# A cached attention decode step with a small MLP: the order of the three weight loads and of the products on them, and the place of TensorE's wait at the end of its group loop

## The chip, the cores and the metric

The kernel runs on one core of a Trainium2 chip. The metric is the device time of one execution in microseconds (us). TensorE (PE in the profile, with its sequencer PEq and its weight loads PEld) does the matrix products, VectorE (DVE) transposes, reductions and elementwise work, ScalarE (ACT) the exponentials and other functions, GpSimd (POOL) small set-up and copies, and SyncE (SP) issues nearly all DMAs, in order, on one queue.

## The reference, cut to what matters

```python
xn = _layernorm(x)                               # x: 2 x 1 x 512
q = (xn @ wq)                                    # 32 heads of 128
scores = einsum("bhqd,bhkd->bhqk", q, k) * (Dh ** -0.5)   # caches: 2 x 8 heads x 32768 x 128, bf16
p = _softmax(scores)
o = einsum("bhqk,bhkd->bhqd", p, v)
s = o.reshape(B, Sq, Hq * Dh) @ wo
# the MLP on xn; with one token the first two products meet only shifted-in zeros,
# so x1 = xn and w1, w2 are not needed
h2 = _gelu(_layernorm(x1) @ w3) @ w4             # w3: 512 x 1792, w4: 1792 x 512
out = x + s * _silu(x1 + h2)
```

The K and V caches are 128 MB each (16 pairs of batch and KV head, 8 MB each for K and V), and every byte is read once.

## The kernel before

**Groups.** A group is one pair of batch and KV head; there are NG = 16. For each group 8 MB of K and 8 MB of V are loaded. K lies in kbuf, which has three slots of 4 MB: even groups use slots 0 and 1, odd ones 1 and 2, so that a new K can start when the first half of the group before is done. V lies in vbuf, one buffer of 8 MB.

**One group.** VectorE transposes K in 16 pieces (L621) into four buffers T and gives one credit on the semaphore `t_vt` for each. TensorE takes two credits at a time (L728, the helper `take` of L404: wait until the semaphore has n, then subtract n), and multiplies each piece with the group's q columns (`z`, L733), in an inner loop of two halves (L725). Then come the head of the group before (`head_xp`, L700), the row maxima of VectorE (`peak`, L600) and their exchange (L743), the exponentials of ScalarE (L523), their transposes on VectorE (L640), the products with V (L755), the sums (L762), ScalarE's copy of the result to `ob` (L528), and four products that turn it (`head_oT`, L694). `fill` (L707) is an idle product whose result nobody reads. The normalising of a group (`head_on`, L575 to L584, ending with the tile `on`) is done by VectorE within the next group, or, after the last group, at once.

**The loop on TensorE.** The body `pe_groups` (L723 to L768) ends with the products of `head_oT` and a compare-and-branch (L768) with a prefetch hint placed at the body's start (L724). The first thing behind the branch is the inner loop's set-up and the take of two credits on `t_vt`. After the last group TensorE falls through to `pe_output` (L771): it waits for VectorE's `oX_sp` and the last copies of `oX`, does the product `wide` (L773), one fill, takes one credit that VectorE gives with `on` (L586), does `head_xp` and then the products with `wo` (L793, L801), which arrive in six parts.

**What orders the DMAs.** SyncE issues in program order: w3 (L325), wq (L326), w4 (L327), the first K (L328), two small pieces of x (L345), the first V (L482, once `e_h2`, the last product on w4, is done, since w3 and w4 lie in vbuf), four small copies of g (L491), then in turn K of the next group (L500, when TensorE has begun the last piece of the first half, which also says that slot's transposes are done) and V of the next group (L482, when TensorE is done with V of the group before, as ScalarE tells at L527). K and V of the last group are split into halves (L505, L486), and the parts of wo follow (L513, L515). The first K-group that overwrites wq's slot also waits for `e_q`.

**The prologue.** After two layernorms (VectorE, with ScalarE's square roots) four small transposes (L409) give `xT`. Then, in this order on TensorE: 16 products on w3 (the gate, L418), q's 32 products on wq in a loop of eight (L439), 14 products on w4 (L468, L462, L470), and one product that spreads q (L471). On VectorE: the transpose of the gate's products (L422) and the gelu's steps up to `h_bf` (L430, with ScalarE's tanh at L428), q's 16 transposes (L450), `q_sb` (L453), the copy `qr` (L474), from which GpSimd makes `z`, and then the silu `g` (L476, L478) and four memsets (L492 to L495), after which the groups begin.

Of the kernel before, what the change touches and what calls it, by code (L numbers as in the profile page):

```python
# [10 lines left out]
ACT = mybir.ActivationFunctionType  # L11
ALU = mybir.AluOpType
# [10 lines left out]
GELU_C = 0.7978845608028654  # L23
# [108 lines left out]
def kernel(  # L132
# [28 lines left out]
    NB = Dh // 64  # L161
# [5 lines left out]
    NQ = 4  # L167
# [46 lines left out]
    sel = sb("sel", [128, 4, 32], BF16)  # L214
# [107 lines left out]
    with tc.tile_critical(sync_engine=mybir.EngineType.Pool, no_gpsimd_drain=True):  # L322
        nc.scalar.wait_ge(t_shift, n_out).then_inc(t_shift, -n_out)

        sp.op(lambda e: e.dma_start(out=vbuf[:, 0:W4O], in_=B_w3.rearrange("(p k) f -> p (k f)", k=DK)), inc=(d_w3, 16))  # L325
        sp.op(lambda e: e.dma_start(out=kbuf_wq[:, 0:DK * HD], in_=A_wq.rearrange("(p k) f -> p (k f)", k=DK)), inc=(d_wq, 16))  # L326
# [77 lines left out]
        def take(eng, s, n=1):  # L404
            eng.wait_ge(s, n).then_inc(s, -n)  # L405

        treg = qrb[:, :].bitcast(BF16)
        for k in range(DK):
# [2 lines left out]
        e_xT = ve.op(lambda v: v.tensor_copy(  # L411
            out=xT[:, :, :].rearrange("p (s k) b -> p s k b", s=2),
            in_=treg[:, 0:64 * DK].rearrange("p (k s c) -> p s k c", k=DK, s=2)[:, :, :, 0:B]), e)
        FQ = Fdim // NQ
        for k in range(DK):
            for n in range(NQ):
                last = k == DK - 1 and n == NQ - 1
                e = pe.op(lambda t, k=k, n=n: t.matmul(  # L418
                    pro[32 * n:32 * n + B, 0:FQ], lhsT=xT[:, DK + k, :],
                    rhs=w3v[:, k, n * FQ:(n + 1) * FQ].rearrange("p (y f) -> p f y", y=32),  # L420
                    start=(k == 0), stop=(k == DK - 1), tile_position=(0, 32 * n)), e_xT, (d_w3, 16), e_pro0, inc=last)
        e = ve.op(lambda v: v.transpose(out=h4[:, :], in_=pro[:, 0:FQ]), e)  # L422
        e_hf = ve.op(lambda v: v.tensor_copy(
            out=hf[:, :].rearrange("p (f b) -> p f b", b=B), in_=h4[:, :].rearrange("p (f c) -> p f c", c=32)[:, :, 0:B]), e)
        e = ve.op(lambda v: v.tensor_mul(out=x2[:, :], in0=hf[:, :], in1=hf[:, :]), e_hf)
        e = ve.op(lambda v: v.tensor_scalar(out=x2[:, :], in0=x2[:, :], scalar1=0.044715, scalar2=1.0, op0=ALU.mult, op1=ALU.add), e)
        e = ve.op(lambda v: v.tensor_mul(out=inner[:, :], in0=hf[:, :], in1=x2[:, :]), e)
        e = ac.op(lambda v: v.activation(out=th[:, :], in_=inner[:, :], func=ACT.Tanh, scale=GELU_C), e)  # L428
        e = ve.op(lambda v: v.tensor_scalar(out=th[:, :], in0=th[:, :], scalar1=0.5, scalar2=0.5, op0=ALU.mult, op1=ALU.add), e)
        e_hb = ve.op(lambda v: v.tensor_mul(out=h_bf[:, :], in0=hf[:, :], in1=th[:, :]), e)  # L430
        HC = 512 // Dh
        NC = Hq // HC
        QP2 = 2 * HC
# [12 lines left out]
        for c in range(NC // 2):  # L446
# [7 lines left out]
            out=q_sb[:, :, :, :].rearrange("p n e (b h) -> p (n e) b h", b=B),  # L454
            in0=qT[:, :].rearrange("p (h c) -> p c h", c=32)[:, 0:B, :].unsqueeze(1).broadcast_to([128, 2 * NB, B, Hq]),
            in1=cls[:, :, :].rearrange("p n e -> p (n e)").unsqueeze(2).unsqueeze(3).broadcast_to([128, 2 * NB, B, Hq])), e)
        h2 = pro
        W4N = 2

        def w4_part(t, j):  # L460
# [7 lines left out]
        pe.op(lambda t: t.matmul(h2[0:B, :], lhsT=h_bf[:, 0:B], rhs=w4v[:, 0, :], start=True, stop=False), e_hb, (d_w4, 16), inc=False)  # L468
        pe.loop(nc, (FK - 2) // W4N, w4_part)
        e_h2 = pe.op(lambda t: t.matmul(h2[0:B, :], lhsT=h_bf[:, (FK - 1) * B:FK * B], rhs=w4v[:, FK - 1, :], start=False, stop=True))  # L470
        e = pe.op(lambda t: t.matmul(  # L471
            qrb[:, 0:NB * 2 * B * Hq], lhsT=sel[:, :, :].rearrange("p j w -> p (j w)"),
            rhs=q_sb[:, :, :, :].rearrange("p n e c -> p (n e c)"), start=True, stop=True), e_q, e_sel)
        e_qr = ve.op(lambda v: v.tensor_copy(  # L474
            out=qr[:, :, :, :, :].rearrange("p n e b h -> p (n e b h)"), in_=qrb[:, 0:NB * 2 * B * Hq]), e)
# [98 lines left out]
        def head_on(c, par=0, behind=None):  # L574
            nc.vector.tensor_reduce(  # L575
                out=den[:, :], in_=S[:, 0:NPART * rep].rearrange("p (i h) -> p h i", h=rep),
                axis=AX.X, op=ALU.add).wait_op(*sum_of(par), "sem-ge").then_inc(*c.inc(t_d))
            nc.vector.reciprocal(out=rec[:, :], in_=den[:, :]).wait_op(*c.at(t_d), "sem-ge").then_inc(*c.inc(t_d))
            nc.vector.tensor_mul(
                out=recm[:, :, :], in0=rec[:, :].unsqueeze(1).broadcast_to([128, NQ, rep]),  # L580
                in1=sel_h[:, :].unsqueeze(2).broadcast_to([128, NQ, rep])).wait_op(*c.at(t_d), "sem-ge").then_inc(*c.inc(t_d))
            e = c.at(t_d)
            nc.vector.wait_ge(*out_of(par))
            ins = nc.vector.tensor_mul(  # L584
                out=on[:, :, :], in0=oT[:, :].unsqueeze(1).broadcast_to([128, NQ, rep]), in1=recm[:, :, :]).wait_op(*e, "sem-ge")
            ins.then_inc(t_vt if behind else t_on, 1)  # L586
            if behind:
                behind()

# [101 lines left out]
        def head_oT():  # L691
            take(nc.tensor, t_ob)
            for t in range(VT):
                ins = nc.tensor.matmul(  # L694
                    oT[:, :], lhsT=ob[:, t * Dh:(t + 1) * Dh], rhs=sel_o[:, t, :],
                    start=(t == 0), stop=(t == VT - 1))
# [26 lines left out]
        with nc.body("pe_groups", valid_engines=[PE]):  # L723
# [44 lines left out]
            nc.tensor.br_lt(turn, NG, on_true="pe_groups", on_false="pe_output").branch_hint(hint_p)  # L768


        with nc.body("pe_output", valid_engines=[PE]):  # L771
            pe.wait(e_sp, e_oX[NG - 2])
            pe.op(lambda t: t.matmul(  # L773
                wide, lhsT=sel_w[:, :, :].rearrange("p j w -> p (j w)"), rhs=oX_sp[:, :, :, :, :].rearrange("p k b j r -> p (k b j r)"),
                start=True, stop=True))
            fill(1)
            take(nc.tensor, t_vt)
            head_xp()
            for i, (a, c, r0, r1) in enumerate(wo_parts):
                if i == 5:  # L780
                    for n in range(NQ):
# [61 lines left out]
```

## Time and profile before

| what | value |
|---|---|
| median of 3 runs | 657.43 us (655.94, 657.43, 1017.87) |
| the profiled execution, its own time | 658.3 us |
| its span, first to last instruction | 656.5 us |
| mean granted TensorE clock | 0.876 |
| TensorE products, busy | 433.2 us (66%) |
| VectorE, busy | 387.6 us (59%) |
| ScalarE, busy | 39.7 us (6%) |
| DMA packets of SyncE's queue | 280.50 MB, 98.8% of 16 engines' span |

The profiled execution took 658.3 us, 1.8 us more than its span, and lies 0.9 us above the median of the runs. The third run of the row, 1017.87 us, left no profile. A timeline row in the fences below gives the start in us, the duration in us, the engine, the line of the kernel, the operation with its tiles, and in brackets how long the engine had been idle and what ended that. PEq, SPq and ACTq are the sequencers of those engines. A row "DMA to landing" gives the time from an issue's start to the arrival of the last byte.

### The profile page before, as it was taken

How to read it: one execution, taken by the hardware profiler on the slowest of the kernel's cores; microseconds unless marked ns; L12 is line 12 of the kernel's file. 1: busy time of each engine (PE TensorE's matmuls, PEld its weight loads, DVE VectorE, ACT ScalarE, POOL GpSimd, SP SyncE). 2: the span in 40 equal slices, each digit the busy share in tenths (PEclk: the TensorE clock that was granted, in tenths of full speed). 3: DMA queues.
4: the chain of work that ended last, by engine and by line, in shares of the span. 5: the costliest groups of instructions: out<-in, count | busy, mean ns of one | idle time of the engine just before them, and what ended most of it. 6: DMA issues, size and time to landing. Idle time of an engine off the chain costs nothing. (4 is left out here: it accounts for less than half of the span.)

```text
span 656.5 us, 6538 instructions
## 1 busy us (share of the span) xinstructions
PE 433.2 (66%) x2443; PEld 161.9 (25%) x2443; DVE 387.6 (59%) x554; ACT 39.7 (6%) x90; POOL 10.3 (2%) x44
## 2 busy tenths in 40 slices
PE   2737587575858756585775658677574866757975
PEld 0212222222322212232222223222222322222322
DVE  5568293763829367381945739185572918548861
ACT  1010101000010100001010000100000010000100
POOL 1000000000000000000000000000000000000000
PEclk9869889697988969799796988979698996969998
DMA  8999999999999999999999999999999999999995
GB/s 361 437 447 447 435 427 415 447 447 435 423 419 447 447 435 415 427 447 447 435 415 427 447 443 439 415 427 447 439 443 411 431 447 435 447 407 429 431 426 236
DMA packets 6245, 280.52 MB, mean 427 GB/s; under 512 B 730, under 2 KB 868, under 8 KB 1380
## 3 DMA queue, kind: packets, MB, share of 16 engines
q1 hardware_dynamic: 6232, 280.50, 98.8%
q8 instruction: 1, 0.02, 0.0%
q10 hardware_dynamic: 12, 0.00, 0.0%
HBM read 280.50 MB, written 0.00 MB: 427 GB/s over the span
## 5 line engine op out<-in xcount | busy, mean ns | idle before, releaser
L621 DVE STREAM_TRANSPOSE T<-kbuf 128x1024 int32<-128x1024 int32 x256 | 296.5, 1214 | 169.7 <-DMA kbuf<-in_A_k_cache_dram 159.5
L733 PE MATMUL banks<-T,z 128*128 128x512 bf16 x1024 | 276.7, 424 | 163.2 <-PEq L405 161.1
L733 PEld LDWEIGHTS banks<-T,z 128*128 128x128 bf16 x1024 | 99.6, 104 | 333.5 <-issue 245.8
L755 PE MATMUL banks<-vbuf,pt 128*16 128x512 bf16 x1024 | 70.4, 379 | 17.7 <-PEq L405 17.7
L523 ACT ACTIVATE ep<-banks,shift 128x512 bf16<-128x512 f32 x32 | 21.7, 682 | 494.6 <-ACTq L405 494.6
L755 PEld LDWEIGHTS banks<-vbuf,pt 128*16 128x16 bf16 x1024 | 27.3, 88 | 64.9 <-issue 42.7
L600 DVE TENSOR_REDUCE mx<-banks 128x1 f32<-128x512 f32 x32 | 21.5, 672 | 34.4 <-PE xp L700 34.4
L707 PE MATMUL pro<-ob,comb 128*2 128x512 f32 x66 | 33.7, 592 | 0.0
L640 DVE STREAM_TRANSPOSE pt<-ep 128x512 bf16<-128x512 bf16 x32 | 22.7, 708 | 15.0 <-ACT ep L523 15.0
L743 PE MATMUL banks<-mxr,same_h 128*128 128x448 f32 x32 | 15.8, 577 | 18.3 <-PEq L405 18.3
L694 PEld LDWEIGHTS oT<-sel_o,ob 128*128 128x128 f32 x128 | 15.5, 191 | 11.1 <-issue 11.1
L694 PE MATMUL oT<-sel_o,ob 128*128 128x4 f32 x128 | 16.4, 252 | 0.0
L762 PE MATMUL banks<-sm,ones_f 128*128 128x448 f32 x32 | 16.3, 593 | 0.0
L528 ACT COPY ob<-banks 128x512 f32<-128x512 f32 x16 | 9.4, 585 | 78.6 <-ACTq L405 78.6
L439 PE MATMUL banks<-kbuf,xT 128*2 x32 | 9.4, 440 | 4.7 <-PEq L405 3.3
L632 DVE TENSOR_REDUCE shift<-banks 128x1 f32<-128x64 f32 x16 | 3.6, 225 | 14.3 <-PE banks L743 14.3
L545 POOL COPY oX<-oXs 128x4 bf16 (+1 forms) x16 | 3.0, 186 | 552.2 <-POOLq L405 552.2
L450 DVE STREAM_TRANSPOSE T<-banks 32x256 f32<-32x256 f32 x16 | 7.0, 440 | 6.7 <-PE banks L439 6.3
L743 PEld LDWEIGHTS banks<-mxr,same_h 128*128 128x128 f32 x32 | 4.8, 188 | 22.6 <-issue 22.6
L604 DVE TENSOR_SCALAR mxr<-row_of,mx 128x32 f32<-128x32 f32 x32 | 7.7, 242 | 1.1
L707 PEld LDWEIGHTS pro<-ob,comb 128*2 128x2 f32 x66 | 4.2, 84 | 14.0 <-issue 10.4
L409 PE MATMUL qrb<-ident,xs_bf 34*128 34x34 bf16 x4 | 0.3, 198 | 9.9 <-DVE xs_bf L369 9.9
(102 smaller groups left out, 87.4 us busy)
## 6 DMA issues: line engine op xcount, KB each, us to landing
kbuf<-in_A_k_cache_dram SPq DMA_DIRECT2D x2, 4096.0 KB, 22.3
vbuf<-in_A_v_cache_dram SPq DMA_DIRECT2D x2, 4096.0 KB, 21.7
kbuf<-in_A_wq_dram SPq DMA_DIRECT2D x1, 4096.0 KB, 16.7
vbuf<-in_B_w_dram SPq DMA_DIRECT2D x2, 1792.0 KB, 14.0
kbuf<-in_A_wo_dram SPq DMA_DIRECT2D x1, 2048.0 KB, 30.7
kbuf<-in_A_wo_dram SPq DMA_DIRECT2D x3, 512.0 KB, 31.8
kbuf<-in_A_wo_dram SPq DMA_DIRECT2D x1, 384.0 KB
kbuf<-in_A_k_cache_dram SPq DMA_DIRECT2D x15, 27.0
```

The costliest lines, as they stand in the source:

```text
L439: ins = t.matmul(out_c, lhsT=xT[:, k, :], rhs=wq3[:, k, bass.ds(c * 512, 512)], start=(k == 0), stop=(k == DK - 1))
L523: nc.scalar.activation(out=ep[i][:, :], in_=sc[i][:, :], func=ACT.Exp, scale=inv_sqrt_dh, bias=shift[:, :], accum_out=rs[:, i:i + 1]).then ...
L528: nc.scalar.copy(out=ob[:, :], in_=o[:, :]).then_inc(t_ob, 1)
L600: ins = nc.vector.tensor_reduce(out=mx[:, i:i + 1], in_=sc[i][:, :], axis=AX.X, op=ALU.max)
L621: ins = nc.vector.transpose(out=Ts[n % T_BUFS][:, :].rearrange("p (b t k) -> p t b k", b=NB, t=RT), in_=kt[:, r * W:(r + 1) * W].rearrange ...
L640: ins = nc.vector.transpose(out=pt[h][:, :, :].rearrange("p r (t h) -> p t r h", h=rep), in_=ep[order(par).index(h)][:, :].rearrange("p (t ...
L694: ins = nc.tensor.matmul(oT[:, :], lhsT=ob[:, t * Dh:(t + 1) * Dh], rhs=sel_o[:, t, :], start=(t == 0), stop=(t == VT - 1))
L707: nc.tensor.matmul(pro[0:B, :], lhsT=comb[:, 0:B], rhs=ob[:, :], start=True, stop=True)
L733: ins = nc.tensor.matmul(sc2[:, bass.ds(i * 512, 512)], lhsT=z[:, nb, w, zc:zc + 128], rhs=Tb[:, nb, :, w], start=(r == 0 and nb == 0 and ...
L743: nc.tensor.matmul(S[:, NPART * rep:NPART * (rep + SREP * 32)].rearrange("p (s c) -> p s c", s=SREP), lhsT=same_h[:, :], rhs=mxr[:, :, :]. ...
L755: ins = nc.tensor.matmul(o[32 * j:32 * j + VT * rep, :], lhsT=pt[h][:, r, a * VT * rep:(a + 1) * VT * rep], rhs=vt[:, u * VT:(u + 1) * VT, ...
L762: nc.tensor.matmul(S[:, 0:SSUM * NPART * rep].rearrange("p (s c) -> p s c", s=SSUM), lhsT=ones_f[:, :], rhs=sm[:, :, :].rearrange("p i h - ...
```

## The change

Three edits. First, in the prologue SyncE issues wq before w3 (then w4, as before). Second, the gate's block (w3's products, its transpose and the gelu) moves behind q's block; q's spreading product and the copy `qr`, which stood behind w4's products, move up to between the gate's products and the gate's VectorE steps. Third, TensorE waits for two credits on `t_vt` ahead of the loop branch, without taking them; the take at the start of the body stays. So that the last group passes too, VectorE gives two credits with `on` there. In `pe_output` the wait for `oX_sp` and `oX` moves onto the product `wide`, the take of the (now two) credits and `head_xp` come ahead of the fill.

```diff
+        sp.op(lambda e: e.dma_start(out=kbuf_wq[:, 0:DK * HD], in_=A_wq...), inc=(d_wq, 16))
         sp.op(lambda e: e.dma_start(out=vbuf[:, 0:W4O], in_=B_w3...), inc=(d_w3, 16))
-        sp.op(lambda e: e.dma_start(out=kbuf_wq[:, 0:DK * HD], in_=A_wq...), inc=(d_wq, 16))
         sp.op(lambda e: e.dma_start(out=vbuf[:, W4O:W4O + FK * D], in_=B_w4...), inc=(d_w4, 16))
...
-        (the gate's block: 16 products on w3, transpose, e_hf, x2, inner, th, e_hb)
         (q's block: loop of products on wq, transposes, e_q)
+        FQ = Fdim // NQ
+        for k in range(DK):
+            for n in range(NQ):
+                last = k == DK - 1 and n == NQ - 1
+                e_h4 = pe.op(lambda t, k=k, n=n: t.matmul(
+                    pro[32 * n:32 * n + B, 0:FQ], lhsT=xT[:, DK + k, :],
+                    rhs=w3v[...], start=(k == 0), stop=(k == DK - 1), ...), e_xT, (d_w3, 16), e_pro0, inc=last)
+        e = pe.op(lambda t: t.matmul(qrb[:, 0:NB * 2 * B * Hq], lhsT=sel..., rhs=q_sb..., start=True, stop=True), e_q, e_sel)
+        e_qr = ve.op(lambda v: v.tensor_copy(out=qr..., in_=qrb[:, 0:NB * 2 * B * Hq]), e)
+        e = ve.op(lambda v: v.transpose(out=h4[:, :], in_=pro[:, 0:FQ]), e_h4)
+        (e_hf, x2, inner, th, e_hb as they were)
...
         e_h2 = pe.op(lambda t: t.matmul(h2[0:B, :], ...))
-        e = pe.op(lambda t: t.matmul(qrb..., lhsT=sel..., rhs=q_sb...), e_q, e_sel)
-        e_qr = ve.op(lambda v: v.tensor_copy(out=qr..., in_=qrb...), e)
...
-            ins.then_inc(t_vt if behind else t_on, 1)
+            ins.then_inc(*((t_vt, 2) if behind else (t_on, 1)))
...
             head_oT()
+            nc.tensor.wait_ge(t_vt, 2)
             nc.tensor.br_lt(turn, NG, on_true="pe_groups", on_false="pe_output").branch_hint(hint_p)
...
         with nc.body("pe_output", valid_engines=[PE]):
-            pe.wait(e_sp, e_oX[NG - 2])
             pe.op(lambda t: t.matmul(
                 wide, lhsT=sel_w..., rhs=oX_sp...,
-                start=True, stop=True))
+                start=True, stop=True), e_sp, e_oX[NG - 2])
+            take(nc.tensor, t_vt, 2)
+            head_xp()
             fill(1)
-            take(nc.tensor, t_vt)
-            head_xp()
```

More of the change, by code (lines that the diff above doesn't have):

```diff
@@ L413 @@
             in_=treg[:, 0:64 * DK].rearrange("p (k s c) -> p s k c", k=DK, s=2)[:, :, :, 0:B]), e)
[L414 to L430, printed above, removed]
         HC = 512 // Dh
@@ L456 @@
             in1=cls[:, :, :].rearrange("p n e -> p (n e)").unsqueeze(2).unsqueeze(3).broadcast_to([128, 2 * NB, B, Hq])), e)
+        FQ = Fdim // NQ
[4 more added lines that the diff above has]
+                    pro[32 * n:32 * n + B, 0:FQ], lhsT=xT[:, DK + k, :],
+                    rhs=w3v[:, k, n * FQ:(n + 1) * FQ].rearrange("p (y f) -> p f y", y=32),
+                    start=(k == 0), stop=(k == DK - 1), tile_position=(0, 32 * n)), e_xT, (d_w3, 16), e_pro0, inc=last)
+        e = pe.op(lambda t: t.matmul(
+            qrb[:, 0:NB * 2 * B * Hq], lhsT=sel[:, :, :].rearrange("p j w -> p (j w)"),
+            rhs=q_sb[:, :, :, :].rearrange("p n e c -> p (n e c)"), start=True, stop=True), e_q, e_sel)
+        e_qr = ve.op(lambda v: v.tensor_copy(
+            out=qr[:, :, :, :, :].rearrange("p n e b h -> p (n e b h)"), in_=qrb[:, 0:NB * 2 * B * Hq]), e)
+        e = ve.op(lambda v: v.transpose(out=h4[:, :], in_=pro[:, 0:FQ]), e_h4)
+        e_hf = ve.op(lambda v: v.tensor_copy(
+            out=hf[:, :].rearrange("p (f b) -> p f b", b=B), in_=h4[:, :].rearrange("p (f c) -> p f c", c=32)[:, :, 0:B]), e)
+        e = ve.op(lambda v: v.tensor_mul(out=x2[:, :], in0=hf[:, :], in1=hf[:, :]), e_hf)
+        e = ve.op(lambda v: v.tensor_scalar(out=x2[:, :], in0=x2[:, :], scalar1=0.044715, scalar2=1.0, op0=ALU.mult, op1=ALU.add), e)
+        e = ve.op(lambda v: v.tensor_mul(out=inner[:, :], in0=hf[:, :], in1=x2[:, :]), e)
+        e = ac.op(lambda v: v.activation(out=th[:, :], in_=inner[:, :], func=ACT.Tanh, scale=GELU_C), e)
+        e = ve.op(lambda v: v.tensor_scalar(out=th[:, :], in0=th[:, :], scalar1=0.5, scalar2=0.5, op0=ALU.mult, op1=ALU.add), e)
+        e_hb = ve.op(lambda v: v.tensor_mul(out=h_bf[:, :], in0=hf[:, :], in1=th[:, :]), e)
         h2 = pro
```

7 lines of the change are left out of this document (1 added, 6 removed).

## The prediction

> **What bounds the kernel now.** I read the page first: the span, the DMA line, the queues and the chain that ended last.
>
> ```profile
> span 656.5 us, 6538 instructions
> DMA  8999999999999999999999999999999999999995
> q1 hardware_dynamic: 6232, 280.50, 98.8%
> q8 instruction: 1, 0.02, 0.0%
> DMA kbuf<-in_A_wo_dram 5%; SPq L515 0%; PE pro L801 0%; PE pro L783 0%; SPq L486 0%; SPq L513 0%; DVE sg L681 0%; DVE out L682 0%; ACTq L527 0%
> ```
>
> SyncE's queue keeps the 16 DMA engines at work for 98.8% of the span; only the first and the last slice show less than nine tenths, and the chain that ended last is the stream's tail (wo) with a few products behind it. TensorE and VectorE have idle time in every group. So the kernel is one stream of 280.5 MB from start to end. Idle DMA time is at most 656.5 x 1.2% = 7.9 us, 1.2% of the time: no reordering can gain more than that while the bytes and the rate stay. An edit costs time only if it makes the stream run dry, or lengthens what follows the last byte.
>
> Next the waits of SyncE's queue and the rows about one group, for how far the issues run ahead of the stream.
>
> ```profile
> SPq L482 <- ACTq L527: 275.4, 14, 19.7
> SPq L500 <- PE banks L733: 251.3, 14, 19.1
> 73.66 0.33 SPq L482 DMA_DIRECT2D vbuf<-in_A_v_cache_dram  x1
> 91.83 0.33 SPq L500 DMA_DIRECT2D kbuf<-in_A_k_cache_dram  x1
> 111.91 0.33 SPq L482 DMA_DIRECT2D vbuf<-in_A_v_cache_dram  x1
> 119.00 5.83 DVE L621 STREAM_TRANSPOSE T<-kbuf 128x1024 int32<-128x1024 int32 x5 [11.14 <-DMA kbuf<-in_A_k_cache_dram]
> DMA to landing us min/median/max: 25.9/26.3/26.9
> ```
>
> SyncE waits for TensorE (L733) before each K and for ScalarE's word that the products on V are done (L527) before each V. V of group 1 is issued at 73.66 and lands 26.3 later, at 100.0; the K behind it was issued at 91.83, so it stood in the queue for 8.1 us. V of group 2 is issued at 111.91, and the K ahead of it lands at 119.00: 7.1 us ahead. What of this is needed for a transfer to get going is bounded below.
>
> **The weights and the prologue.** SyncE issues the same bytes, so the first K lands where it did; what moves is wq, w3, and with them the order of the products.
>
> ```profile
> 0.90 0.40 SPq L325 DMA_DIRECT2D vbuf<-in_B_w_dram  x1
> DMA to landing us min/median/max: 7.5/7.5/7.5
> 1.36 0.41 SPq L326 DMA_DIRECT2D kbuf<-in_A_wq_dram  x1
> DMA to landing us min/median/max: 16.7/16.7/16.7
> 12.06 3.41 PE L418 MATMUL pro<-vbuf,xT 128*2 128x448 bf16 x16 [1.89 <-DVE xT L411]
> 15.52 0.65 DVE L422 STREAM_TRANSPOSE T<-pro 128x448 f32<-128x448 f32 x1 [3.60 <-PE pro L418]
> 17.55 0.19 DVE L430 TENSOR_TENSOR h_bf<-hf,th 128x28 bf16<-128x28 f32 x1
> 18.80 5.31 PE L439 MATMUL banks<-kbuf,xT 128*2 x16 [3.33 <-PEq L405]
> 28.55 1.02 PE L439 MATMUL banks<-kbuf,xT 128*2 x4 [0.34 <-issue]
> 29.41 0.38 PE L468 MATMUL pro<-vbuf,h_bf 128*2 128x512 bf16 x1
> 29.61 1.85 DVE L450 STREAM_TRANSPOSE T<-banks 32x256 f32<-32x256 f32 x4 [0.86 <-PE banks L439]
> 31.50 0.59 DVE L453 TENSOR_TENSOR q_sb<-T,cls 128x256 bf16<-128x256 f32 x1
> 34.12 0.38 PE L470 MATMUL pro<-vbuf,h_bf 128*2 128x512 bf16 x1
> 34.43 0.28 PE L471 MATMUL qrb<-q_sb,sel 128*128 128x256 bf16 x1
> 34.53 0.36 SPq L482 DMA_DIRECT2D vbuf<-in_A_v_cache_dram  x1
> 34.75 0.42 DVE L474 CAST qr<-qrb 128x256 bf16<-128x256 f32 x1 [2.66 <-PE qrb L471]
> 38.34 0.48 DVE L495 MEMSET pro<- 128x512 f32 x1
> 41.73 5.84 DVE L621 STREAM_TRANSPOSE T<-kbuf 128x1024 int32<-128x1024 int32 x5 [2.91 <-DMA kbuf<-in_A_k_cache_dram]
> ```
>
> w3 lands at 0.90 + 7.5 = 8.4 and wq at 1.36 + 16.7 = 18.1, 9.7 us behind it for 4.19 MB (433 GB/s). The 1.835 MB of w3 take 4.2 us at that rate, so the stream begins in effect at 8.4 - 4.2 = 4.2. With wq first it lands at 4.2 + 9.7 = 13.9, w3 at 18.1, and w4 and K where they were.
>
> Then step by step. q's first product starts 0.7 us behind wq's landing (18.1 to 18.80), at 14.6; xT is there at 12. The loop ran from 18.80 to 29.57, 10.8 us, so it ends at 25.4. The gate's 16 products need w3, there since 18.1: 3.4 us, to 28.8. Meanwhile VectorE turns the last of q (29.61 to 32.09 before, now 25.4 to 27.9). The spreading product no longer waits: 28.8 to 29.1, and `qr` (0.4) is done at 29.5. VectorE is in order, so the gate's transpose stands behind it: from 29.5 the chain up to `h_bf` takes what it took (15.52 to 17.74, 2.2 us), to 31.7. The products on w4 took 29.41 to 34.50, 5.1 us, and TensorE has nothing else to do: 31.8 to 36.9. The first V is thus issued at about 36.9, and 34.53 before: **2.4 us later**. The first K holds the stream until 41.73, so V is issued 4.8 us ahead instead of 7.2. `qr` is ready 5.7 us earlier (29.5 for 35.2), but the groups wait for K at 41.73 in either order, and the gain is nothing. g, the four copies of it on SyncE and the memsets move 2.4 us too: the last memset ends at 38.82 + 2.4 = 41.2, still ahead of K; SyncE's next K waited until 53.7 anyway. Were VectorE late there, the first group would start late, which the 7 us ahead of the stream take up.
>
> What a new transfer needs to get going has no row in mid-stream. Bounds: nothing (its descriptors stand ready behind K's), and the 3.3 us from the first issue at 0.90 to 4.2. I take the upper end, since it is the only start from an empty queue that the trace has: 36.9 + 3.3 = 40.2, 1.5 us ahead of the end of K. Cost nothing; if that cover is gone, each us costs one.
>
> **The loop branch.** Before, the branch ran while TensorE waited; now it runs after the second credit and lies ahead of the group's first product.
>
> ```profile
> L768 PEldq COMPARE_BRANCH  x16: 76/227/228, 74.5 to 643.9; - x16
> L724 PEldq BRANCH_PREFETCH_HINT  x16: 40/40/50, 39.1 to 615.1; - x16
> L725 PEldq MOVE  x48: 29/29/35, 39.2 to 622.0; - x48
> ```
>
> Taken it is 0.227 us, not taken 0.076. With the hint (0.040) and two or three of the moves (0.029 each) a group's first product starts 0.3 to 0.4 us later; all behind it, K's next issue, the exponentials, the products on V and V's next issue, moves by as much. 15 passes x 0.35 = 5.3 us if nothing covered it. But the issues are 8.1 and 7.1 us ahead, 4.8 and 3.8 beyond the 3.3 us of a start, and the delay does not add up over the groups, since each begins when its K lands and not when the one before ends. So nothing. The wait holds nothing else up: what stands behind it on TensorE is that same take.
>
> **The tail.** After the last group the branch waits for `on`, and the product `wide` behind it too.
>
> ```profile
> 644.84 1.02 PE L707 MATMUL pro<-ob,comb 128*2 128x512 f32 x2
> 644.95 0.18 DVE L584 TENSOR_TENSOR on<-oT,recm 128x16 bf16<-128x16 f32 x1 [0.51 <-PE oT L694]
> 645.91 1.04 PE L793 MATMUL qrb<-kbuf,T 128*2 128x512 bf16 x16
> 648.08 0.39 PE L793 MATMUL qrb<-kbuf,oX 128*2 128x512 bf16 x4 [0.90 <-DMA kbuf<-in_A_wo_dram]
> 651.84 0.81 PE L801 MATMUL pro<-kbuf,oXz 128*4 128x128 bf16 x12 [2.14 <-DMA kbuf<-in_A_wo_dram]
> ```
>
> `on` ends at 645.1; with the branch, `wide`, `head_xp` and the fill of 1.0 us the products on wo's first part start at about 646.7 instead of 645.91. They and the next part's need 1.4 us and end at 648.1, when the third part lands as before (648.08). From there each product waits for its DMA, the last at 651.84. Up to 3 us later would still be taken up by those waits. Nothing again.
>
> **Sum.** 658.3 + 0 + 0 + 0 = 658.3 against the profiled execution. The median of the runs is 0.9 lower, so I forecast 657.5.
>
> **Rivals.**
> (a) The first V is issued too late. If the gate's chain or w4's products run slower than here (TensorE's clock is granted at half at times), V comes after 38.4 and the stream stops between the first K and V, 1:1. At 3 us later than worked out, 1.5 us of idle; at 6 us, 4.5: 659 to 662. For: only 1.5 us of cover. Against: every step has a row.
> (b) Slower: the taken branch must fetch code, and only now does that lie ahead of a group. The place is L768's branch, the price a stall S in each of 15 passes; it decides once S is over the 3.8 us of cover, and is over 2% (13.1 us) at S = 3.8 + 13.1 / 15 = 4.7. Were the code to queue behind the V then in flight (19 us), it would be 15 x 15.2 = 228 us, a time near 885. On a queue of its own it would be like this small load, issued at 1.06 and used at 4.29, 3.2 us, which is covered:
>
> ```profile
> 1.06 0.55 ACTq L333 DMA_DIRECT2D x_bf<-in_A_x_dram  x1
> 4.29 0.42 DVE L351 CAST shared<-x_bf 2x512 f32<-2x512 bf16 x1 [0.53 <-DMA x_bf<-in_A_x_dram]
> ```
>
> Against it: the queue of instructions moved one packet of 0.02 MB in the whole span, where 15 passes would need 15.
> [...]
> (c) Faster by over 2%: only a higher DMA rate could, as idle time is 1.2%. Some 2.5% more would give 642. Nothing in the rows speaks for it; the loads are the same.
> (d) The change does what it says but nothing of it reaches the end: that is my forecast.
>
> **How the numbers follow.** Forecast 0.76, (a) 0.13, (b) 0.08, (c) 0.03. The first two lie within 2% (about what a measurement of this kernel can tell from no change), 0.89 together; slower by over 2% is (b), faster (c). The range of 655 to 662 holds the forecast with the spread of the two near runs (655.94, 657.43), a little below, and (a)'s upper end; it leaves out (b) and (c), 0.11.
>
> **What would show it.** In the changed profile: q's products from about 14.6, the gate's at 25.4, w4's from 31.8, the first V's issue at 36.9, the first K's landing still at 41.7 and the second K's use where it was; the take of the group's first credits 0.3 to 0.4 us further behind the second transpose; DMA still near 98.8%; the products on wo's first part at 646.7 and the last at 651.8. A DMA share under 98%, more packets on the instruction queue, or a first V issue after 38.4 would prove me wrong.

## The result and the profile after

| | before | after |
|---|---|---|
| median of 21 runs each | 656.75 us (655.86 to 1017.87) | 655.57 us (655.26 to 657.22) |
| ratio of the times, 95% interval | | 0.9982 [0.9975, 0.9989] |
| the profiled execution, its own time | 658.3 us | 655.5 us |
| its span | 656.5 us | 653.7 us |
| mean granted TensorE clock | 0.876 | 0.885 |

The ratio leaves out the one run of 1017.87 us. The changed kernel is faster by 0.7 to 1.6 us of 656.75 (one minus the ends of the interval), 1.2 us in the middle. That is small, but it is clear of zero, and the prediction had set it at nothing. The two profiled executions lie 2.8 us apart, since the one of before is among the later of its runs. The spread is part of the result: 14 of the 20 other runs of before took more than 656.35 us, and 1 of 21 after. Such a run is called late below. The limit lies in a gap of those 20 runs, none of which took 656.10 to 656.42 us; after the change the shortest runs lie 0.6 us lower (655.26 for 655.86), and the same limit is kept.

The page of the kernel after, the lines that answer to the first fence of the prediction:

```profile
span 653.7 us, 6538 instructions
DMA  8999999999999999999999999999999999999997
q1 hardware_dynamic: 6232, 280.50, 99.2%
q8 instruction: 1, 0.02, 0.0%
```

The bytes, the packets and the one packet of the instruction queue are the same; the busy share is higher (99.2% for 98.8%) because the same work lies in a shorter span. The prologue, from the timeline of the kernel after (start, duration, engine, line, operation):

```profile
0.90 0.40 SPq L325 DMA_DIRECT2D kbuf<-in_A_wq_dram  x1
13.91 8.36 PE L422 MATMUL banks<-kbuf,xT 128*2 x24 [2.51 <-PEq L405]
24.91 3.38 PE L444 MATMUL pro<-vbuf,xT 128*2 128x448 bf16 x13
31.24 0.58 PE L473 MATMUL pro<-vbuf,h_bf 128*2 128x512 bf16 x1 [2.73 <-DVE h_bf L461]
37.08 0.36 SPq L482 DMA_DIRECT2D vbuf<-in_A_v_cache_dram  x1
40.92 5.84 DVE L621 STREAM_TRANSPOSE T<-kbuf 128x1024 int32<-128x1024 int32 x5
```

The view of line L325 in the same trace, from the issue of wq to its landing:

```profile
DMA to landing us min/median/max: 12.2/12.2/12.2
```

wq lands at 0.90 + 12.2 = 13.1, q's products start at 13.91, the gate's end at 28.3, w4's run from 31.24, and the first V is issued at 37.08: 2.55 later than before. All of it lies within 0.8 us of what was forecast. The first K is off by as much (40.9 for 41.7), and it was forecast not to move at all.

The tail is where the time goes. The chain of waits of the kernel before, in order of time (start, length, what it was):

```profile
616.73 34.98 DMA kbuf<-in_A_wo_dram
...
651.84 0.81 PE pro L801 x12
652.65 0.85 PE pro L783 x8
653.50 0.23 PE pro L801 x4
```

The same of the kernel after:

```profile
616.93 32.80 DMA kbuf<-in_A_wo_dram
...
649.86 0.50 PE pro L801 x12
650.36 0.44 PE pro L783 x8
650.80 0.13 PE pro L801 x4
```

The twelve products wait for the fifth part of wo, the four behind them for the sixth and last. The fifth is reported landed at 649.72 instead of 651.71, 2.0 us earlier, and the products behind it take 1.07 instead of 1.89 us, 0.8 less. Together that is the 2.8 us between the two spans. The shorter products have the granted clock behind them; the stretches of one us, first of before, then of after (length, busy time of PE, PEld, DVE, ACT and POOL with counts, then the granted clock, the DMA share and GB/s):

```profile
650.00:651.00 1.00, 0.00 (x0) 0.00 (x0) 0.00 (x0) 0.34 (x1) 0.00 (x0) 0.83 0.08 17
651.00:652.00 1.00, 0.16 (x4) 0.19 (x6) 0.00 (x0) 0.00 (x0) 0.00 (x0) 0.50 0.03 11
652.00:653.00 1.00, 1.00 (x18) 0.84 (x16) 0.00 (x0) 0.00 (x0) 0.00 (x0) 0.50 0.00 0
```

```profile
649.00:650.00 1.00, 0.41 (x10) 0.17 (x8) 0.00 (x0) 0.59 (x1) 0.00 (x0) 1.00 0.45 155
650.00:651.00 1.00, 0.91 (x24) 0.66 (x19) 0.05 (x1) 0.00 (x0) 0.00 (x0) 1.00 0.00 0
```

Before, the DMA engines stand nearly idle (17 and 11 GB/s) for two us while TensorE waits for wo. A stream that has run out on nearly every engine is waiting for one of them, and the packets of the trace tell which. Their records don't name an engine; what ran on one is told by the times, as each piece begins where the one before it ended. On the engine that fetched the one packet of the instruction queue, 16384 bytes (start, us, bytes; kernel before):

```
649.38  0.93  16384   the instruction packet
650.30  0.34   3072   wo, fifth part
650.62  0.34   3072
650.94  0.21   3072
651.15  0.12   3072
651.27 to 651.61: eight of 1024, 0.05 each, wo, sixth part
```

Four pieces of the fifth part and all eight of the sixth stood behind that 0.93 us packet, and the first ones behind it took 0.34 us instead of 0.12. They end at 651.27 and 651.61, while the other 15 engines are done with the fifth part by 649.89 and with the sixth by 650.23. After the change the packet runs from 649.69 to 650.62, no piece of wo is behind it on its engine, and the two parts end at 649.45 and 649.79 on all 16. So of the last byte's 1.82 us (651.61 to 649.79), 1.38 are the packet (651.61 to 650.23), and 0.44 belong to the other 15.

There is a second difference in the packets, and it holds all through the stream. Each of the 16 engines carries a sixteenth of every load, for the most part in pieces of 64 KB that take 2.42 us each (3840 of them, 240 for each engine). A round is here the next 16 of them to end. In the first round the latest engine ends 0.94 us behind the middle one before, and 0.23 after; in the last of the 240 rounds, 0.86 and 0.40. The middle engine ends its last piece at the same time, 600.75 and 600.77; the latest at 601.61 and 601.17, which is the 0.44 again. Lateness from the first loads is carried to the end.

### The profile page after: what moved, and what is told of

Read it like the earlier page. It is cut to its first block, busy times and chain, and to the rows that moved or that the text cites. A ratio compares the mean times of both kernels' runs of the same rounds, so it can differ in the third digit from the quotient of the medians.

```text
span 653.7 us, 6538 instructions
## 1 busy us (share of the span) xinstructions
PE 433.5 (66%) x2443; PEld 162.0 (25%) x2443; DVE 388.0 (59%) x554; ACT 39.7 (6%) x90; POOL 10.3 (2%) x44
## 3 DMA queue, kind: packets, MB, share of 16 engines
q1 hardware_dynamic: 6232, 280.50, 99.2%
## 5 line engine op out<-in xcount | busy, mean ns | idle before, releaser
L733 PEld LDWEIGHTS banks<-T,z 128*128 128x128 bf16 x1024 | 99.2, 103 | 332.0 <-issue 244.0
## 6 DMA issues: line engine op xcount, KB each, us to landing
kbuf<-in_A_wq_dram SPq DMA_DIRECT2D x1, 4096.0 KB, 12.2
```

The lines of the kernel that those rows point to most:

```text
L733: ins = nc.tensor.matmul(sc2[:, bass.ds(i * 512, 512)], lhsT=z[:, nb, w, zc:zc + 128], rhs=Tb[:, nb, :, w], start=(r == 0 and nb == 0 and ...
```

## The experiments

The first theory was that the loads bring the gain: with wq first the engines start more evenly, and the latest engine ends earlier. Its rival was the tail: the wait and the new order around it. After four runs the second had a mechanism, the instruction packet that meets the end of wo, and two readings of what moves it: that TensorE's work comes later, or that it leaves the loop later. Each result is the median in us with the lowest and the highest run, and the ratio to runs of the kernel before on the same chip, whose medians were 656.43 to 656.74; 68 of these 113 runs were late.

**The loads alone.** Before, with wq ahead of w3:

```diff
+        sp.op(lambda e: e.dma_start(out=kbuf_wq[:, 0:DK * HD], in_=A_wq...), inc=(d_wq, 16))
         sp.op(lambda e: e.dma_start(out=vbuf[:, 0:W4O], in_=B_w3...), inc=(d_w3, 16))
-        sp.op(lambda e: e.dma_start(out=kbuf_wq[:, 0:DK * HD], in_=A_wq...), inc=(d_wq, 16))
```

> The kernel before with wq issued ahead of w3, and nothing else changed. Theory S (skew of the DMA engines): in the trace of before three of the 16 engines get their first packet at 3.7 to 3.9 us instead of 1.9 to 2.3, and the latest engine stays 0.86 us behind the middle one in every round of 64 KB packets up to 601 us; in the changed kernel all start by 2.6 and it is 0.40. So this kernel should have the whole gain: 0.9975 to 0.999 of before (about 1.2 us less), with the first K landing at about 40.9 us instead of 41.7 and all engines started by 2.6. Rival W (the wait ahead of the branch and the new order in the tail bring the gain): 1.000. Rival Q (the order of the products brings it): 1.000.

656.88 (655.25 to 658.0, 12 runs), ratio 1.0003 [0.9992, 1.0013]. No gain in the median. But three runs lie at 655.25 to 655.41, lower than any of the 35 of before beside them (655.82 at the lowest), and nine are late. In the profiled run, one of the three, the latest engine is 0.41 behind in the first round and 0.32 in the last. So the loads lower the floor by some 0.5 us, and something else puts most runs above it.

**The change, but with w3 first.** After, with w3 ahead of wq again and the order of the products left as changed:

```diff
-        sp.op(... A_wq ...)
         sp.op(... B_w3 ...)
+        sp.op(... A_wq ...)
```

> The changed kernel with the two loads back in the old order (w3 first), so the order of the products, the wait and the tail stay changed. q's products now wait for wq at 18.1 us, so the last product on w4 should end near 41.2 and the first V be issued there, 0.5 us ahead of the end of the first K. Theory S: the gain is gone, and the stream has a gap of 0 to 3 us between the first K and V: a transfer issued into an empty queue had its first packet 1.0 us behind the issue (0.90 to 1.93), so about 1 us of gap, ratio 1.000 to 1.004. Rivals W and Q: the gain stays but for that gap, 0.998 to 1.002.

658.66 (657.82 to 659.81, 11 runs), ratio 1.0032 [1.0021, 1.0042]. The timeline of that kernel:

```profile
41.58 0.36 SPq L482 DMA_DIRECT2D vbuf<-in_A_v_cache_dram  x1
...
57.24 0.36 SPq L500 DMA_DIRECT2D kbuf<-in_A_k_cache_dram  x1
```

q's products wait for wq, which now comes second, and the gate's and w4's wait behind q's. The first V is issued at 41.58, 4.5 later than with wq first. From the packets: K's last pieces end at 40.1 to 41.5, V's first begin at 42.57 to 43.00, and by the 15th round the engines are 2.9 to 3.0 us behind those of the changed kernel (the first ends at 60.09 for 57.10). This is the rival (a) of the prediction, made real by another edit. The new order of the products needs wq first.

**The wait alone.** Before, with the wait ahead of the branch, two credits with `on`, and the new order of `pe_output`:

```diff
-            ins.then_inc(t_vt if behind else t_on, 1)
+            ins.then_inc(*((t_vt, 2) if behind else (t_on, 1)))
...
+            nc.tensor.wait_ge(t_vt, 2)
             nc.tensor.br_lt(turn, NG, on_true="pe_groups", on_false="pe_output").branch_hint(hint_p)
...
             (pe_output as in the change)
```

> The kernel before with the wait ahead of the loop branch, the two credits with on, and the new order in the tail, but the old loads and products. Theory S: 1.000, three engines start late again, and a group's first product comes about 0.55 us further behind the second transpose without any effect. Rival W: 0.998.

656.00 (655.74 to 656.29, 11 runs), ratio 0.9989 [0.9979, 0.9998]; no run is late. The instruction packet starts at 650.25, behind wo's fifth part (650.02). The latest engine is still 1.21 behind in the first round and 1.09 in the last, so this gain has nothing to do with the loads.

**The change without the wait.** After, with the branch, the credits and `pe_output` as before (the edit above taken back):

> The changed kernel without the wait ahead of the branch, with one credit from on and the old order in the tail. Theory S: all of the gain stays, 0.9975 to 0.999. Rival W: 1.000.

657.61 (655.55 to 658.0, 11 runs), ratio 1.0009 [0.9998, 1.0019]; ten are late. From its chain of waits, in order of time:

```profile
616.03 34.74 DMA kbuf<-in_A_wo_dram
...
650.91 0.81 PE pro L801 x12
```

The products take 0.81 again. The instruction packet is at 648.74 to 649.68 here, with pieces of wo behind it on its engine until 650.6. With wq first the latest engine is little behind (0.34, then 0.27), and the time is lost all the same. So the two edits bring two different things, and without the wait that of the loads doesn't show in the median.

**The loads, and a later TensorE.** Wq first, the products and the branch as before, and one idle product more ahead of the second half of V in each group:

```diff
-    FILL = (1, 1)
+    FILL = (1, 2)
```

> The kernel with only the loads changed (wq first), and one more idle product per group ahead of the second half of V (2 passes of 0.43 us). What the four runs so far show: a page of 16 KB of instructions is fetched once, 4.8 to 5.0 us behind the last group's head_oT, through one of the 16 DMA engines (0.93 us); where that engine still has pieces of wo to bring, the last part of wo lands up to 1.5 us late, TensorE idles for 2 us and its clock falls to half for the last products. Theory F (the fetch collides with the end of wo): the wait ahead of the branch helps because it makes the last group's chain 0.57 us later, so that the fetch comes when that engine is done. Then 0.86 us more in the chain by an idle product does the same without the wait: all runs within 655.2 to 656.0, ratio 0.998 to 0.999. Rival T (the order in the tail, or the wait itself, keeps TensorE's clock up): the spread of the loads-only kernel stays, 655.3 to 658.0, ratio 1.000 to 1.001.

655.70 (655.32 to 657.99, 11 runs), ratio 0.9979 [0.9968, 0.999]; two are late. The gain comes without the wait, by a TensorE that leaves its loop at 645.8 and not at 643.7 as with the loads alone. That is 2.1 us later, where the idle product was expected to add 0.86. The profiled run is one of the two late ones, and its chain shows what a late one looks like:

```profile
617.89 33.54 DMA kbuf<-in_A_wo_dram
...
651.57 0.76 PE pro L801 x12
```

Its instruction packet starts at 649.42, and wo's sixth part ends at 651.15. So a later loop makes the collision rare, not impossible.

**The change with a shorter group.** After, without the idle product there:

```diff
-    FILL = (1, 1)
+    FILL = (1, 0)
```

> The changed kernel without the idle product ahead of the second half of V: the last group's chain 0.86 us earlier, the wait ahead of the branch and the tail's order kept. Theory F: the fetch comes 0.9 us earlier, into the last parts of wo, and most runs are 656.4 to 658: ratio 1.000 to 1.002. Rival T: as the changed kernel, 0.998.

656.28 (655.8 to 656.97, 11 runs), ratio 0.9989 [0.998, 0.9999]; five are late, none by much. Theory F had expected most runs at 656.4 to 658. The exit moves only from 645.3 to 644.8, since the last group's chain came 0.5 us earlier and not 0.86 (`on` ends at 644.76, and at 645.24 in the kernel after). Two rows of its timeline:

```profile
649.98 0.50 PE L801 MATMUL pro<-kbuf,oXz 128*4 128x128 bf16 x12 [0.61 <-DMA kbuf<-in_A_wo_dram]
...
651.79 0.28 PE L801 MATMUL pro<-kbuf,oXz 128*4 128x128 bf16 x4 [0.88 <-DMA kbuf<-in_A_wo_dram]
```

The packets of wo are all there by 649.88, but the last four products wait until 651.79. The instruction packet runs from 649.74 to 650.67. Each engine ends its share of a part with a packet of 4 bytes, by its place the write that reports the share. On 15 engines it is through by 649.89; the last one starts at 650.65, just as the instruction packet ends. The last update of the part's semaphore comes at 651.75, and the products follow. So this time the report was held up, and not the data.

**A shorter start.** The loads alone, and the gate with 4 products in place of 16 (three quarters of its sum left out), to shift the prologue:

```diff
-        for k in range(DK):
+        for k in range(1):
             for n in range(NQ):
-                    start=(k == 0), stop=(k == DK - 1), ...
+                    start=True, stop=True, ...
```

> The kernel with only the loads changed, and the gate's products cut from 16 to 4 (its result is wrong by that), so that TensorE's program is 12 products shorter ahead of the loop. It asks whose fetch it is: if TensorE's sequencer asks for the page when it passes a certain place in its program, that place moves behind the products on wo's first part, and the fetch comes later or not at all, with all runs near 655.3 (ratio 0.998 to 0.999). If another engine or a fixed place in the code asks for it, the fetch stays at 4.7 to 4.9 us behind head_oT and the spread at 655.3 to 658.0 (ratio 1.000 to 1.001). Theory T expects the latter too.

657.48 (656.26 to 658.05, 11 runs), ratio 1.001 [1.0001, 1.002]; ten are late. The exit is at 643.3 and the packet starts at 648.87. Both are 0.3 us earlier than in the loads alone (643.7 and 649.19), so a shorter prologue does not hold the packet back, and the runs are as late. In the three kernels with wq first and neither the wait nor a longer group (this one, the loads alone, the change without the wait) 29 of 34 runs are late, against 68 of 113 in before. The order of the loads doesn't make late runs rarer; its lower floor shows in the median only where something else does.

**The wait with the old tail.** Before, with the wait and two credits, while `pe_output` keeps its order:

```diff
+            nc.tensor.wait_ge(t_vt, 2)
...
-            take(nc.tensor, t_vt)
+            take(nc.tensor, t_vt, 2)
```

> The kernel before with the wait ahead of the branch and the two credits alone; loads, products and the order of the fill and head_xp in the tail as before. Theory F: as with the new order in the tail, no collision, all runs within 655.7 to 656.4, ratio 0.999. Rival T by the tail's order: the spread of before, 655.8 to 658.3, ratio 1.000.

655.98 (655.66 to 657.17, 11 runs), ratio 0.9989 [0.9978, 1.0]; three are late. The median is that of the wait with the new tail (656.00). The order of `pe_output` brings nothing that these runs can tell, though three late runs stand against none there.

**The new tail alone.** Before, with the order of `pe_output` as changed, one credit, no wait:

```diff
-            pe.wait(e_sp, e_oX[NG - 2])
             pe.op(lambda t: t.matmul(wide, ...,
-                start=True, stop=True))
-            fill(1)
+                start=True, stop=True), e_sp, e_oX[NG - 2])
             take(nc.tensor, t_vt)
             head_xp()
+            fill(1)
```

> The kernel before with the new order in the tail alone (the wait of the product wide on its own instruction, head_xp ahead of the fill), no wait ahead of the branch. Theories F1 and F2: the spread of before, 655.8 to 658.3, ratio 1.000. Rival T (the order keeps TensorE's clock up): 0.999, all runs under 656.4.

656.56 (655.98 to 658.3, 12 runs), ratio 0.9995 [0.9984, 1.0005]; eight are late, as in before. It is the wait, not the tail.

**The change with an early exit.** After, but in the last group VectorE gives the two credits that the wait asks for before it starts on the normalising, by a write of zeros to `recm`, which is written anew behind it; `on` gives the third, which `pe_output` takes:

```diff
+        ve.op(lambda v: v.memset(recm[:, :, :], 0.0), inc=(t_vt, 2))
...
-            ins.then_inc(*((t_vt, 2) if behind else (t_on, 1)))
+            ins.then_inc(t_vt if behind else t_on, 1)
...
-            take(nc.tensor, t_vt, 2)
+            take(nc.tensor, t_vt, 3)
```

> The changed kernel, but VectorE gives the two credits that let TensorE out of the loop as soon as it leaves its own loop itself (about 639 us), and on gives a third, which the take ahead of head_xp waits for. The wait ahead of the branch, and with it the 0.57 us on each group's first product, stay; what goes is the 0.9 us by which TensorE left the loop later in the last group. Theory F2 (the fetch of the 16 KB page is asked for when TensorE leaves its loop; the wait holds that back until the last pieces of wo are all in their engine's queue): TensorE leaves at about 644.3 instead of 645.3, and collisions come back in part, as in the kernel without the idle product (which left at 644.8, 0.5 us earlier by the stream): half or more of the runs above 656.2, ratio 0.9985 to 1.0005. Theory F1 (the fetch is tied to the chain of the last group, and the 0.57 us do it): all runs 655.2 to 656.0, ratio 0.998.

656.94 (655.52 to 657.98, 12 runs), ratio 0.9998 [0.9988, 1.0009]; eight are late. The branch of that kernel (count, then ns at least, in the middle and at most, first and last time):

```profile
L770 PEldq COMPARE_BRANCH  x16: 76/228/228, 82.2 to 644.5; - x16
```

All of the change is in, and only the last exit is moved, from 645.3 to 644.5. The gain is gone.

**The loads and the wait.** After, with the products of the prologue in their old order:

> The kernel before with the loads wq, w3, w4 and the wait ahead of the branch with its tail, but the products in the old order (the gate's first). Theory S+F (the skew of the DMA engines by the loads, the collision by the wait; the order of the products brings nothing): as the changed kernel, nearly all runs 655.2 to 655.9, ratio 0.998. If the order of the products brings something of its own, this one is slower than the changed kernel by that: 0.9985 or more.

655.56 (655.35 to 656.03, 12 runs), ratio 0.9977 [0.9968, 0.9987]; none is late. This is the changed kernel's median without the edit of the products. From its chain of waits:

```profile
616.57 32.89 DMA kbuf<-in_A_wo_dram
...
649.60 0.50 PE pro L801 x12
```

**A late exit by other means.** After, with the products of the prologue in their old order, and the branch waiting on a semaphore of its own: GpSimd gives a credit in each group when the next `z` is made, and VectorE gives the last one with `on`:

```diff
+            nc.gpsimd.sem_inc(t_x, 1)          (in GpSimd's loop, behind put_z(m + 1))
...
-            ins.then_inc(*((t_vt, 2) if behind else (t_on, 1)))
+            ins.then_inc(t_x if behind else t_on, 1)
...
-            nc.tensor.wait_ge(t_vt, 2)
+            take(nc.tensor, t_x)
...
-            take(nc.tensor, t_vt, 2)
```

> The kernel with the loads wq, w3, w4, where TensorE takes a credit of a semaphore of its own ahead of the loop branch: GpSimd gives it in the middle of each group but the last, so that it never waits there, and VectorE gives the last one with on. So the last exit from the loop is held back until on is done, as in the changed kernel, while no group's first product is delayed (0.30 instead of 0.87 us behind the second transpose). Theory F2 (when TensorE leaves its loop decides whether the fetch of the page hits the end of wo): exit near 644.6 to 645.0 instead of 643.7, and few or none of the runs above 656.35, median 655.4 to 655.9, ratio 0.9975 to 0.9985. If the delay of the groups counts beside it, the exit is 0.5 us earlier than in the changed kernel by the stream, and a part of the runs is late: median 656.0 to 656.8.

655.44 (655.23 to 656.88, 12 runs), ratio 0.9984 [0.9973, 0.9995]; two are late. The loop's first products of group 1 and the loop's branch, first in the kernel after, then in this one:

```profile
79.88 4.62 DVE L621 STREAM_TRANSPOSE T<-kbuf 128x1024 int32<-128x1024 int32 x4 [11.77 <-DMA kbuf<-in_A_k_cache_dram]
83.10 9.59 PE L733 MATMUL banks<-T,z 128*128 128x512 bf16 x32 [9.15 <-PEq L405]
...
L769 PEldq COMPARE_BRANCH  x16: 76/228/228, 82.3 to 645.3; - x16
```

```profile
79.84 4.62 DVE L622 STREAM_TRANSPOSE T<-kbuf 128x1024 int32<-128x1024 int32 x4 [11.39 <-DMA kbuf<-in_A_k_cache_dram]
82.50 3.81 PE L734 MATMUL banks<-T,z 128*128 128x512 bf16 x10 [8.21 <-PEq L405]
...
L770 PEldq COMPARE_BRANCH  x16: 88/234/234, 73.5 to 645.5; - x16
```

In the kernel after, the branch first runs at 82.3, behind the second credit, and the first product starts 3.22 us behind K's first transpose; here it runs at 73.5, while K is still under way, and the product starts after 2.66. Only the last exit is held, to 645.5, and the gain is there in full. So the delay within the groups costs nothing that shows, and what the wait does at the last exit brings all that the wait brings.

## Why the prediction was wrong

**Where it failed.** The prediction took the end of the stream as fixed: "what moves is wq, w3, and with them the order of the products", with K where it was, and in the tail "the last at 651.84 ... Nothing again". It asked of each edit whether it delays the stream or what lies behind it, and never whether it moves the last landing. The last landing moved, by both edits:

- *The wait, 0.4 to 0.75 us with w3 first.* The run with the wait alone has 656.00, the runs of before on its chip 656.44, those of the first comparison 656.75; by the ratio (0.9989) it is 0.7. Without the wait the sequencer reaches the last branch 0.73 us ahead of the last `head_oT` product (643.86 and 644.59 before; 643.16 and 643.89 in the change without the wait). With it the branch stands behind `on`: in the kernel after, `on` ends at 645.24 and the branch runs at 645.28. The one packet of the instruction queue, at 649.38 before and 649.69 after, is then mostly no longer ahead of the last pieces of wo on its DMA engine. Where it was, in before, the last byte came 1.4 us later (above), and the products behind it took 0.8 us longer (1.89 for 1.07). Shown: the wait alone gains, the change without it doesn't, the early exit takes the gain away, and a late exit by another semaphore brings it. The packets agree, with one profile for each kernel: where the exit is at 644.2 or before (five profiles) the packet starts at 648.7 to 649.7, where it is later (eight, leaving out the change with w3 first, whose stream is 3 us behind) at 649.4 to 651.2. Pieces of wo end behind the packet in before, the change without the wait, the longer group, the shorter start and the new tail alone, whose profiled runs are all late, and in none of the seven profiled runs that aren't. That the late runs without a profile have the same cause is inferred.
- *The order of the loads, some 0.45 us where the wait is there (656.00 to 655.56, the wait with w3 first and with wq first).* The two ran on different occasions; by the ratios to their own runs of before (0.9989 and 0.9977) it would be 0.8 us, and the intervals overlap. The packets of the two profiled executions say 0.44. With w3 first the latest engine was 0.94 to 1.21 us behind in the first round in all five profiles of such kernels, with wq first 0.23 to 0.41 in all nine; in four of the five it was still 0.84 to 1.09 behind at the last round. The fifth is the change with w3 first, where the gap at the first V brought the engines together (0.25 at the last). The last piece of 64 KB of the stream is that of the latest engine: 601.61 before and 601.17 after, with the middle one at 600.75 and 600.77.

The two steps add up to the 1.2 us between the medians because they run from the one median over 656.00 to the other; that is no check. In the other order the loads alone bring nothing (ratio 1.0003), and the wait behind them 1.3 us (656.88 to 655.56, again on different occasions). The edit of the products brings nothing that shows (655.56 without it, 655.57 with it).

**The number.** The forecast of 657.5 lies 1.9 us above the 655.57 measured. 0.7 of this is the start: the forecast went by the three runs of before, whose median was 657.43, and over 21 runs it is 656.75. The other 1.2 is the change, set at nothing. The range of 655 to 662 reached below for the spread of two runs, and that the result fell into it is luck.

**The bound on the page.** "Idle DMA time is at most 7.9 us" held and covers the gain; the mistake was to read 98.8% as a stream with nothing left in it for an edit that adds no bytes. The share is a mean over 16 engines, and the time went by the last one (done with wo at 651.61 in before, the other 15 by 650.23).

**The prologue.** Every step came within 0.8 us: V issued at 37.08 for 36.9, and covered, as forecast. The start of a transfer that nothing showed was bounded by 0 and 3.3 us and set at 3.3. The change with w3 first measures it: V issued at 41.58 and its first packet at 42.57, 1.0 us. The cover was thus 2.0 us (37.08 + 1.0 against 40.1, where the first engine ends K's pieces in the kernel after), where 1.5 was forecast. That the first K stands ready 0.8 us earlier (40.92 for 41.73) was not forecast: VectorE starts on it 0.36 us behind the end of its last piece (40.56 to 40.92; before, 0.37 us, 41.36 to 41.73), and the latest engine was 0.7 us less behind (0.23 for 0.94), which is most of the 0.8.

**The branch.** Forecast 0.3 to 0.4 us later for a group's first product and hidden. It is 0.55 (3.22 us behind the first transpose against 2.67 before), and hidden: the late exit without that delay is no faster than the change by more than the spread of the runs (655.44 and 655.57).

**The tail.** The first products on wo came at 646.62 (forecast 646.7), the twelve behind the fifth part at 649.86 (forecast 651.8). That the wait holds the exit back was counted as a cost, taken up by the waits for wo. The rows for the other reading stood in the quoted fences, unused: the products behind the fifth part waited 2.14 us for their DMA where those behind the third had waited 0.90 (and those behind the fourth 0.85, by the same timeline).

**The rivals.** None came. For (b), the one packet of the instruction queue was rightly read as proof that no pass fetches code; that a taken branch fetches any, as (b) supposed, no run shows. But the question of when that one packet ran, and what stood behind it, wasn't asked, and that is what the wait changed. The packet has 16384 bytes. After, at 649.69 to 650.62, no piece of wo stands behind it, and before, at 649.38 to 650.31, it put off the last byte by 1.38 us.

**What stays open.** Which engine asks for the instruction packet, and at which instruction. From the last exit to the fetch it is 5.50 to 5.58 us in before, the loads alone, the new tail alone, the change without the wait, the shorter start, and the loads with the wait; but 4.41 after, 4.44 with the wait alone, 3.66 with the longer group, 6.74 with the early exit, and 4.15 to 5.19 in the other four. So the exit is not all that sets the fetch's time. Late runs remain with the longer group, the old tail and the other semaphore (two or three of 11 or 12 each), and the profiled run of the early exit, which isn't late, has its packet at 651.22. In the profiles with the longer and the shorter group the middle engine ended its last piece of 64 KB 0.4 us later than after (601.18 and 601.16 for 600.77), with 102 and 81 pieces over 2.45 us where the kernel after has 15, so these two runs moved the stream as well, and why isn't known. Why w3 ahead of wq spreads the engines is open too: in before three of the 16 began their first large packet at 3.75 to 3.85 us and the others at 1.9 to 2.3, but with the wait alone all had begun by 2.7, and the latest was 1.21 behind all the same. There three of the pieces begun at 2.6 to 2.7 took 1.7 to 1.9 us, where most later ones took 0.54; that these put their engines behind is likely, but not followed up.

## What to carry to other kernels

In a kernel that is one stream, as here, the end follows the last piece on the last DMA engine (651.61 before, 649.79 after): compare the engines' ends in the first round and the last, and look at what else, such as an instruction packet (0.93 us here), uses an engine in the last microseconds. A wait that costs nothing on its own engine can still shift such a packet (649.38 before, 650.25 with the wait alone), for better or worse. And look at all runs, not at the median alone: two clusters 1 to 2 us apart can be a race, and an edit that changes how often it is lost moves the median without making any instruction faster.

## What the runs showed of the hardware

- Lateness of a DMA engine stayed through 577 us of a full stream, where in before all but 3 of the 3840 pieces of 64 KB took at most 2.45 us and the middle one 2.42, so that a late engine didn't catch up: 0.94 us at the first round and 0.86 at the last before, 1.21 and 1.09 with the wait alone. The gap of the stream in the change with w3 first brought the engines together (1.08 to 0.40 across the late first V).
- One instruction packet of 16384 bytes held a DMA engine for 0.93 us in before and in after, and in before the first two pieces just behind it took 0.34 us instead of 0.12. With the shorter group the 4-byte packet of the last part, held until 650.65 by such a packet, led to the semaphore's last update 1.1 us later (651.75); before, it took 0.4 (651.61 to 652.02).
- TensorE's granted clock fell to 0.50 in the wait of 2.14 us at the end of before, at about 650.66 by the mean of 0.83 in that us, which is 0.95 us after its last product; in the wait of 0.59 us of the kernel after it stayed at 1.00. In the 3.66 us from 647.00 to 650.66 TensorE was busy for 0.95 us before, and for 2.28 us after, where the clock stayed. No run varied the wait alone, so what sets the fall is not shown.
